# Every instruction tied to its predecessor in the source: the planned order becomes each engine's order

## The chip, the cores and the metric

The kernel runs on one core of a Trainium2 chip. A core has a matrix engine (PE, whose weight loads are listed apart as PEld), a vector engine (DVE), an activation engine (ACT), a general engine (POOL), and a queue engine (SP). Each runs its own stream of instructions in the order in which they stand in that stream, and semaphores tie the streams together. Transfers between the chip's large memory and the on-chip memory are issued from POOL's stream (loads) and from SP's (stores). The metric is the device time of one execution in microseconds. Lower is better.

## The reference

Two steps follow each other. The first is attention with a symmetric window of 32 positions, for 8 batches of 8 heads, 576 positions and head dimension 64. The second routes each of the 4608 resulting rows of 512 values to its two best of eight low-rank adapters and adds their result to the row.

```python
scores = scale * np.matmul(q, k.transpose(0, 1, 3, 2))
mask = np.abs(pos[:, None] - pos[None, :]) <= window          # window = 32
attn = softmax(np.where(mask, scores, -1e9))                  # over the last axis
x = np.matmul(attn, v)   # (B, H, S, D) -> rows (B*S, H*D) = (4608, 512)
logits = x @ w_gate                                           # 8 adapters
topk = two largest logits of a row; w = softmax of those two
delta[row] = sum over the two e of  w_e * ((x[row] @ A[e]) @ B[e])   # rank 16
out = x + delta                                               # float32
```

## The kernel before, in words

The work is cut into small tasks with two-letter names, each one function of the kernel. `b` counts the 8 batches, `n` the 4 head pairs of a batch (unit `u = 4b + n`), `t` the three load tiles of a batch, `w` is 0 for q and 1 for k, `T` counts 36 score tiles of 8 blocks (4.5 a batch), and `h` is one of three row groups of a batch.

- Loads, issued from POOL's stream: `LD` (L274) brings one tile of q or k, `LV` (L279) one half of v. Between them POOL also runs the memsets of `init_v` and `init_kq` and the loads of the weights, at fixed places after the 4th, 8th, 10th and 16th load.
- DVE: `RG` (L289) copies a loaded tile into the layout that is transposed next (tile `c` from tile `l`), `SV` (L284) moves a half of v into place (tile `vbd`), `MU` (L350, L351) divides an attention product by its row sums into `x`, `XE` (L369) copies the transposed x out of PSUM into `xT`, `G1` and `G2` (L394 to L415) are the routing, and `OB` (L446) copies one of the three output groups.
- PE: `TR` (L297) transposes a copied tile, `SC` (L317, L323) computes a score tile with its mask, `PV` (L341) multiplies by v, `TX` (L363) transposes x, `PZ` (L377) computes logits and the first adapter product, `TZ` (L422) transposes the gated result, and `PD` (L432, L435) makes the second adapter product plus x.
- ACT: `EQ` (L303) and `EK` (L311, two copies) take the transposed q and k out of PSUM, `EX` (L328) is the exponential of a score tile, `GA` (L402) the exponential of the gate, `ZE` (L426) a copy, and `OB` (L444) copies two output groups of a batch.
- Stores `ST` (L452) are issued from SP's stream.

PSUM is used as three wide buffers W and two narrow ones T. A task that fills one waits until the task before it on that buffer has been read. There are seven load buffers for each of q and k (a load waits for the `RG` of the tile seven places before it) and three v buffers (a load of v waits for the products of the batch three before it).

`plan()` is a small list scheduler in the kernel's own Python. With a table of costs, the due times of `OFF` and the buffers above it makes one list of all tasks, `order`, and gives each PSUM task its buffer. The kernel then calls the task functions in that list's order, so the source order of instructions is the plan's order. That is not yet the order in which an engine runs them: when the tile framework's context ends, its own scheduler sorts each engine's instructions by its own estimate of when their inputs are ready, as far as data dependencies allow. Only that sorted order reaches the chip. The loop that traces the instructions is

```python
    for t in order:
        do[t.key[0]](*t.key[1:])
```

Of the kernel before, what the change touches and what calls it, by code (L numbers as in the profile page):

```python
# [23 lines left out]
J = 8  # L24
# [206 lines left out]
def kernel(  # L231
# [10 lines left out]
    nc = tc.nc  # L242
    assert tuple(q.shape) == (B, H, S, D)
# [28 lines left out]
    def LD(b, w, t):  # L272
        src = (q, k)[w][b].rearrange("(o n) (p j) d -> (n p) o (j d)", o=2, j=J)
        nc.gpsimd.dma_start(out=raw[w][(NT3 * b + t) % NRAW], in_=src[FT * t:FT * t + FT])  # L274

    def LV(b, o):
        src = v[b, 4 * o:4 * o + 4].rearrange("n (a p two) d -> p (n a) (two d)", p=32, two=2)
        p0, c0 = 64 * o, VW * o + V0
        nc.gpsimd.dma_start(out=vbd[b % NV][p0:p0 + 32, :, c0:c0 + 2 * D], in_=src)  # L279

    def SV(b, o):
        d = vbd[b % NV]
        p0, c0 = 64 * o, VW * o + V0
        nc.vector.tensor_copy(out=d[p0 + 32:p0 + 64, :, c0:c0 + D],  # L284
                              in_=d[p0:p0 + 32, :, c0 + D:c0 + 2 * D])
# [14 lines left out]

    def EQ(b, t):
        c0 = QP + J * FT * t
        nc.scalar.copy(  # L303
            out=qTs[b % 2][:, c0:c0 + J * FT].rearrange("p (f j) -> p f j", j=J),
            in_=ps("TR", b, 0, t)[:, 0:J * FT].rearrange("p (j f) -> p f j", j=J))

    def EK(b, t):
        kt = ps("TR", b, 1, t)[:, 0:J * FT].rearrange("p (r j a f) -> p a r f j", r=2, j=4, f=8)
        for o in range(2):
            dst = kTs[b % 2][64 * o:64 * o + 64, BT * t:BT * t + BT, 64 * o:64 * o + 64]  # L310
            nc.scalar.copy(out=dst.rearrange("p a (r f j) -> p a r f j", r=2, j=4),  # L311
                           in_=kt[64 * o:64 * o + 64])

    def SC(T):
        p = ps("SC", T).rearrange("p (i c) -> p i c", c=128)
        for i in range(0, TB, 4):
            nc.tensor.matmul(out=p[:, i:i + 4], lhsT=maskT, rhs=bcast(ident, 1, 4),  # L317
                             start=True, stop=False)
        for i in range(TB):
            u, a = divmod(TB * T + i, NB)  # L320
            b, n = divmod(u, NP)
            c0 = S * n + 64 * a
            nc.tensor.matmul(  # L323
                out=p[:, i], lhsT=kTs[b % 2][:, NB * n + a, :],
                rhs=qTs[b % 2][:, c0:c0 + 128], start=False, stop=(i % 4 == 3))

    def EX(T):
        nc.scalar.activation(out=PTs[T % NPT][:, :, 64:192],  # L328
                             in_=ps("SC", T).rearrange("p (i c) -> p i c", c=128),
                             func=AF.Exp, scale=1.0 / float(D) ** 0.5)  # L330

    def PV(u):
        b, n = divmod(u, NP)
        po = ps("PV", u)
        for g in range(NG):
            ops = [(a, off) for a, off in ((2 * g - 1, 128), (2 * g, 64), (2 * g + 1, 0))
                   if 0 <= a < NB]
            for i, (a, off) in enumerate(ops):
                T, sl = divmod(NB * u + a, TB)
                rhs = vbd[b % NV][:, NB * n + a].rearrange("p (o c) -> p o c", o=2)  # L340
                nc.tensor.matmul(  # L341
                    out=po[:, GS * g:GS * g + 2 * VD], lhsT=PTs[T % NPT][:, sl, off:off + 128],
                    rhs=rhs[:, :, V0 - 1:V0 + D], start=(i == 0), stop=(i == len(ops) - 1))

    def MU(u):
# [12 lines left out]
    def TX(b, h):  # L358
        tp = ps("TX", b, h)
        for g in gs(h):  # L360
            for c in range(4):
                c0 = 512 * (g % 2) + 128 * c
                nc.tensor.matmul(out=tp[:, c0:c0 + 128],  # L363
                                 lhsT=xs[b % NX][:, g, 128 * c:128 * c + 128],
                                 rhs=ident, is_transpose=True, start=True, stop=True)

    def XE(b, h):
        n = len(gs(h))
        nc.vector.tensor_copy(  # L369
            out=xTs[b % NXT][:, 2 * h:2 * h + n].rearrange("p g c k -> p (g c k)"),  # L370
            in_=ps("TX", b, h)[:, 0:512 * n])

    def PZ(b):
        xT, pz = xTs[b % NXT], ps("PZ", b)
        for g in range(NG):
            for c in range(4):
                nc.tensor.matmul(out=pz[:, GS * g:GS * g + ER + E],  # L377
                                 lhsT=xT[:, g, c, :], rhs=WA_sb[:, c, :],
                                 start=(c == 0), stop=(c == 3))
# [6 lines left out]
    def G1(b):  # L386
        lg = zview(b)[:, :, ER:ER + E]

        def sm(name, shape):
# [4 lines left out]
        nc.vector.tensor_reduce(out=m1, in_=lg, axis=AX.X, op=ALU.max)  # L394
        nc.vector.tensor_tensor(out=is1, in0=lg, in1=bcast(m1, 2, E), op=ALU.is_ge)
        nc.vector.scalar_tensor_tensor(out=lm, in0=is1, scalar=-1e30, in1=lg,
                                       op0=ALU.mult, op1=ALU.add)
        nc.vector.tensor_reduce(out=m2, in_=lm, axis=AX.X, op=ALU.max)
        nc.vector.tensor_tensor(out=dm, in0=m2, in1=m1, op=ALU.subtract)

    def GA(b):
        nc.scalar.activation(out=st[b, "dm"], in_=st[b, "dm"], func=AF.Exp)  # L402

    def G2(b):
# [4 lines left out]
        nc.vector.tensor_tensor(out=is2, in0=lm, in1=bcast(m2, 2, E), op=ALU.is_ge)  # L409
        nc.vector.tensor_scalar(out=s, in0=dm, scalar1=1.0, scalar2=None, op0=ALU.add)  # L410
        nc.vector.reciprocal(out=s, in_=s)
        nc.vector.tensor_tensor(out=is2, in0=is2, in1=bcast(dm, 2, E), op=ALU.mult)  # L412
        nc.vector.tensor_tensor(out=gate, in0=is1, in1=is2, op=ALU.add)
        nc.vector.tensor_tensor(out=gate, in0=gate, in1=bcast(s, 2, E), op=ALU.mult)
        nc.vector.tensor_tensor(  # L415
            out=zss[b % 2], in0=zview(b)[:, :, 0:ER].rearrange("p g (e r) -> p g e r", r=R),
            in1=bcast(gate, 3, R), op=ALU.mult)

    def TZ(b):
        zs = zss[b % 2].rearrange("p g e r -> p g (e r)")  # L420
        for g in range(NG):
            nc.tensor.matmul(out=ps("TZ", b)[:, 128 * g:128 * g + 128], lhsT=zs[:, g],  # L422
                             rhs=ident, is_transpose=True, start=True, stop=True)

    def ZE(b):
        nc.scalar.copy(out=zTs[b % 2].rearrange("p g k -> p (g k)"),  # L426
                       in_=ps("TZ", b)[:, 0:640])

    def PD(b, h):
        pd = ps("PD", b, h).rearrange("p (i c) -> p i c", c=DD)  # L430
        for i, g in enumerate(gs(h)):
            nc.tensor.matmul(out=pd[:, i], lhsT=zTs[b % 2][:, g], rhs=B_sb,  # L432
                             start=True, stop=False)
            for c in range(4):
                nc.tensor.matmul(out=pd[:, i, 128 * c:128 * c + 128],  # L435
                                 lhsT=xTs[b % NXT][:, g, c], rhs=ident,
                                 start=False, stop=(c == 3))

    def OB(b, h):
# [3 lines left out]
        if ts["OB", b, h].eng == "ACT":  # L443
            nc.scalar.copy(out=dst, in_=src)  # L444
        else:
            nc.vector.tensor_copy(out=dst, in_=src)  # L446

    def ST(b, h):
        for i, g in enumerate(gs(h)):
            lo, hi = (32 if g == 0 else 0), (96 if g == NG - 1 else 128)  # L450
            r0 = S * b + 128 * g - 32
            nc.sync.dma_start(out=out[r0 + lo:r0 + hi], in_=obs[(3 * b + h) % NOB][lo:hi, i])  # L452
# [11 lines left out]
    def constants():  # L464
        make_identity(nc, ident)
        nc.gpsimd.memset(mask, 0.0)
        nc.gpsimd.affine_select(out=mask, in_=mask, compare_op=ALU.is_ge, fill=NEG,
                                base=0, channel_multiplier=1,
                                pattern=[[0, 2], [-1, 2], [-2, 32]])
        nc.gpsimd.affine_select(out=mask, in_=mask, compare_op=ALU.is_ge, fill=NEG,  # L470
                                base=64, channel_multiplier=-1,
                                pattern=[[0, 2], [1, 2], [2, 32]])

    def init_kq(i, eng):
        eng.memset(kTs[i][0:64, :, 64:128], 0.0)
        eng.memset(kTs[i][64:128, :, 0:64], 0.0)
        eng.memset(qTs[i][:, 0:QP], 0.0)
        eng.memset(qTs[i][:, QP + NP * S:], 0.0)

    def init_v(i, eng):  # L480
        eng.memset(vbd[i][0:64, :, VW + V0 - 2:VW + V0 + D], 0.0)
        eng.memset(vbd[i][64:128, :, V0 - 2:V0 + D], 0.0)
        eng.memset(vbd[i][0:64, :, V0 - 1:V0], 1.0)
        eng.memset(vbd[i][64:128, :, VW + V0 - 1:VW + V0], 1.0)
# [16 lines left out]
    nc.vector.memset(qTs[0][:, QP + S * 1:QP + S * 1 + 32], 0.0)  # L501
# [49 lines left out]
```

## Time and profile before

| | us |
|---|---|
| median of 3 timed runs | 205.47 (202.04 to 207.04) |
| the profiled execution | 199.97 |
| its span, first to last instruction | 198.0 |
| PE busy, 1720 matmuls | 137.4 (69% of the span) |
| PEld busy | 110.5 (56%) |
| DVE busy | 114.2 (58%) |
| ACT busy | 114.5 (58%) |
| POOL busy | 65.7 (33%) |

All views are of the profiled execution, and their times run from its first instruction. In a timeline each row is a start, a duration, the engine, the line of the kernel, the operation, and out<-in. A bracket names the idle time of the engine just before, and what ended it. Buffer numbers are left out in these views.

### The profile page before, as it was taken

To read this page: it belongs to the slowest core of one execution; us is meant where nothing else is said; L and a number is where in the kernel's file an instruction comes from. 1 tells how busy PE (TensorE), PEld (TensorE's weight loads), DVE (VectorE), ACT (ScalarE), POOL (GpSimd) and SP (SyncE) were. 2 spreads that over 40 slices of the span, in tenths; PEclk is the share of its full clock that TensorE was granted. 3 is DMA by queue.
4 is the path that set the end of the run, shared out by engine and by line. 5 is a ranking of instruction groups with operands and counts; after the bars stand their busy time and mean duration, and the time that the engine had idled before them with its cause. 6 is when DMAs were issued, how large, how long until landed. Compare 5 with 4: busy or idle time off the path is not lost. (4 is left out here: it accounts for less than half of the span.)

```text
span 198.0 us, 4213 instructions
## 1 busy us (share of the span) xinstructions
PE 137.4 (69%) x1720; PEld 110.5 (56%) x1720; DVE 114.2 (58%) x273; ACT 114.5 (58%) x141; POOL 65.7 (33%) x91
## 2 busy tenths in 40 slices
PE   0058395546688655695777979896789899789380
PEld 0046183435586444673565767675667867667250
DVE  6899029060458503956397569377585976676601
ACT  1047900663504975476649867976959899345241
POOL 7999979956202800206220612150000000000000
PEclk9999958585569999789999999999999999999955
DMA  4994999799991996134992499589414006006606
GB/s 65 159 138 75 128 166 42 103 182 197 181 135 9 135 159 158 27 52 78 211 175 46 95 164 257 87 135 255 52 60 181 4 0 239 2 2 237 243 14 224
DMA packets 38770, 24.12 MB, mean 122 GB/s; under 512 B 24800, under 2 KB 34144, under 8 KB 38752
## 3 DMA queue, kind: packets, MB, share of 16 engines
q0 software_dynamic: 33504, 14.43, 64.9%
q1 hardware_dynamic: 5248, 9.44, 13.7%
q8 instruction: 13, 0.21, 0.5%
q14 instruction: 5, 0.04, 0.1%
HBM read 28.85 MB, written 9.44 MB: 193 GB/s over the span
## 5 line engine op out<-in xcount | busy, mean ns | idle before, releaser
L328 ACT ACTIVATE PT<-W 128x1024 f16<-128x1024 f32 x36 | 36.1, 1025 | 12.5 <-PE W L323 10.6
L341 PE MATMUL W<-vbd,PT 128*128 128x130 f16 x416 | 33.9, 240 | 11.0 <-DVE vbd L284 6.0
L311 ACT COPY kT<-T 64x768 f16<-64x768 f16 x48 | 38.1, 793 | 4.9 <-PE T L297 4.6
L297 PE MATMUL T<-ident,c 96*128 96x96 f16 x384 | 25.6, 220 | 17.5 <-DVE c L289 15.1
L341 PEld LDWEIGHTS <-PT 128*128 128x128 f16 x416 | 29.9, 108 | 12.9 <-issue 8.4
L303 ACT COPY qT<-T 128x768 f16<-128x768 f16 x24 | 19.2, 799 | 30.6 <-PE T L297 27.7
L297 PEld LDWEIGHTS <-c 96*128 96x128 f16 x384 | 21.9, 106 | 24.4 <-DVE c L289 19.3
L369 DVE COPY xT<-T 128x1024 f16<-128x1024 f16 (+1 forms) x24 | 13.9, 600 | 31.0 <-PE T L363 20.0
L323 PE MATMUL W<-qT,kT 128*128 128x128 f16 x288 | 25.4, 229 | 6.1 <-ACT kT L311 5.2
L317 PE MATMUL W<-ident,mask 128*128 128x512 f16 x72 | 24.2, 420 | 6.5 <-ACT PT L328 4.0
L274 POOL DMA_DIRECT2D l<-in_q_dram x24 | 16.6, 690 | 36.3 <-DVE is L412 12.0
L323 PEld LDWEIGHTS <-kT 128*128 128x128 f16 x288 | 20.0, 103 | 12.2 <-ACT kT L311 4.5
L351 DVE TENSOR_TENSOR x<-W,rc 128x640 f16<-128x640 f32 x32 | 26.2, 820 | 0.8
L289 DVE COPY c<-l 96x1024 f16<-96x1024 f16 x48 | 25.8, 573 | 0.3
L350 DVE RECIPROCAL rc<-W 128x10 f32<-128x10 f32 x32 | 6.9, 215 | 27.9 <-PE W L341 23.5
L279 POOL DMA_DIRECT2D vbd<-in_v_dram x16 | 13.5, 845 | 25.4 <-PE W L341 23.2
L444 ACT COPY ob<-W 128x1024 f32<-128x1024 f32 x16 | 16.3, 1016 | 8.5 <-PE W L435 5.7
L432 PE MATMUL W<-B_sb,zT 128*128 128x512 f16 x40 | 16.4, 410 | 3.3 <-ACT ob L444 0.9
L435 PEld LDWEIGHTS <-xT 128*128 128x128 f16 x160 | 13.3, 104 | 8.5 <-issue 4.5
L435 PE MATMUL W<-ident,xT 128*128 128x128 f16 x160 | 17.3, 231 | 0.0
L363 PE MATMUL T<-ident,x 128*128 128x128 f16 x160 | 13.7, 230 | 4.1 <-DVE xT L369 1.5
L274 POOL DMA_DIRECT2D l<-in_k_dram x24 | 15.7, 653 | 2.3 <-DVE c L289 1.7
(55 smaller groups left out, 129.4 us busy)
## 6 DMA issues: line engine op xcount, KB each, us to landing
out_dram<-ob SPq DMA_DIRECT2D x24, 256.0 KB, 2.7
l<-in_q_dram POOLq DMA_DIRECT2D x24, 192.0 KB, 7.0
l<-in_k_dram POOLq DMA_DIRECT2D x24, 192.0 KB, 7.4
vbd<-in_v_dram POOLq DMA_DIRECT2D x16, 288.0 KB, 8.1
out_dram<-ob SPq DMA_DIRECT2D x16, 192.0 KB, 2.4
WA_sb<-in_moe_A_dram POOLq DMA_DIRECT2D x4, 32.0 KB, 7.9
B_sb<-in_moe_B_dram POOLq DMA_DIRECT2D x1, 128.0 KB, 4.8
WA_sb<-in_moe_w_gate_dram POOLq DMA_DIRECT2D x1, 8.0 KB, 5.4
```

What stands on the lines that cost most here:

```text
L274: nc.gpsimd.dma_start(out=raw[w][(NT3 * b + t) % NRAW], in_=src[FT * t:FT * t + FT])
L289: nc.vector.tensor_copy(out=cst[w][i % NCAST], in_=raw[w][i % NRAW].rearrange("p o (j d) -> p j o d", j=J))
L297: nc.tensor.matmul(out=tp[:, FT * slot:FT * slot + FT], lhsT=src[:, j, :], rhs=ident[0:FT, 0:FT], is_transpose=True, start=True, stop=True)
L303: nc.scalar.copy(out=qTs[b % 2][:, c0:c0 + J * FT].rearrange("p (f j) -> p f j", j=J), in_=ps("TR", b, 0, t)[:, 0:J * FT].rearrange("p (j ...
L311: nc.scalar.copy(out=dst.rearrange("p a (r f j) -> p a r f j", r=2, j=4), in_=kt[64 * o:64 * o + 64])
L317: nc.tensor.matmul(out=p[:, i:i + 4], lhsT=maskT, rhs=bcast(ident, 1, 4), start=True, stop=False)
L323: nc.tensor.matmul(out=p[:, i], lhsT=kTs[b % 2][:, NB * n + a, :], rhs=qTs[b % 2][:, c0:c0 + 128], start=False, stop=(i % 4 == 3))
L328: nc.scalar.activation(out=PTs[T % NPT][:, :, 64:192], in_=ps("SC", T).rearrange("p (i c) -> p i c", c=128), func=AF.Exp, scale=1.0 / floa ...
L341: nc.tensor.matmul(out=po[:, GS * g:GS * g + 2 * VD], lhsT=PTs[T % NPT][:, sl, off:off + 128], rhs=rhs[:, :, V0 - 1:V0 + D], start=(i == 0 ...
L351: nc.vector.tensor_tensor(out=xs[b % NX].rearrange("p g (h n d) -> p g h n d", h=2, n=NP)[:, :, :, n], in0=pog[:, :, :, 1:VD], in1=bcast(r ...
L432: nc.tensor.matmul(out=pd[:, i], lhsT=zTs[b % 2][:, g], rhs=B_sb, start=True, stop=False)
L435: nc.tensor.matmul(out=pd[:, i, 128 * c:128 * c + 128], lhsT=xTs[b % NXT][:, g, c], rhs=ident, start=False, stop=(c == 3))
```

## The change

`tc.keep_in_program_order` takes an instruction and adds a scheduling edge to the instruction that was traced before it on the same engine. The edge fixes the order of issue. It adds no semaphore and no wait. The change puts this call around every instruction that the kernel itself emits. The planner, its costs and due times, the buffers and the instructions stay as they were. The two instructions of the helper `make_identity` at the start are not wrapped. One added line moves the later line numbers by one (L289 is L290 in the changed kernel).

```diff
     nc = tc.nc
+    keep = tc.keep_in_program_order
...
     def RG(b, w, t):
         i = NT3 * b + t
-        nc.vector.tensor_copy(out=cst[w][i % NCAST],
-                              in_=raw[w][i % NRAW].rearrange("p o (j d) -> p j o d", j=J))
+        keep(nc.vector.tensor_copy(out=cst[w][i % NCAST],
+                              in_=raw[w][i % NRAW].rearrange("p o (j d) -> p j o d", j=J)))
...
-            nc.tensor.matmul(
+            keep(nc.tensor.matmul(
                 out=tp[:, FT * slot:FT * slot + FT], lhsT=src[:, j, :],
-                rhs=ident[0:FT, 0:FT], is_transpose=True, start=True, stop=True)
+                rhs=ident[0:FT, 0:FT], is_transpose=True, start=True, stop=True))
...
-        nc.vector.reciprocal(out=rc, in_=pog[:, :, :, 0])
-        nc.vector.tensor_tensor(
+        keep(nc.vector.reciprocal(out=rc, in_=pog[:, :, :, 0]))
+        keep(nc.vector.tensor_tensor(
             out=xs[b % NX].rearrange("p g (h n d) -> p g h n d", h=2, n=NP)[:, :, :, n],
-            in0=pog[:, :, :, 1:VD], in1=bcast(rc, 3, D), op=ALU.mult)
+            in0=pog[:, :, :, 1:VD], in1=bcast(rc, 3, D), op=ALU.mult))
...
```

The same wrapping stands in every other task function, in the memsets, and in the weight loads. The order of loads on POOL and of stores on SP is the same before and after. On PE the 180 tasks were run in 225 pieces before (a task cut by another counts as two), and run in 180 whole ones now. On DVE it was 175 pieces and is 144, on ACT 117 and 116.

The first place is on DVE at the start. Names ending in 89 to 91 are copied q tiles (`c`), those in 92 to 94 copied k tiles; `l_3` to `l_6` are the load buffers of batch 1 (3 to 5) and of batch 2's first tile (6). An `rc` row and the `x` row behind it are one `MU`. Before:

```order
L284 COPY vbd_64<-vbd_64 32x36x64
L350 RECIPROCAL rc<-W_107 128x10
L351 TENSOR_TENSOR x_95<-W_107,rc 128x10x64
L350 RECIPROCAL rc<-W_108 128x10
L351 TENSOR_TENSOR x_95<-W_108,rc 128x10x64
L350 RECIPROCAL rc<-W_107 128x10
L351 TENSOR_TENSOR x_95<-W_107,rc 128x10x64
L289 COPY c_0_89<-l_3_78 96x1024
L289 COPY c_0_92<-l_3_85 96x1024
L289 COPY c_1_90<-l_4_79 96x1024
```

The same place on DVE in the changed kernel:

```order
L285 COPY vbd_64<-vbd_64 32x36x64
L290 COPY c_0_89<-l_3_78 96x1024
L290 COPY c_0_92<-l_3_85 96x1024
L351 RECIPROCAL rc<-W_107 128x10
L352 TENSOR_TENSOR x_95<-W_107,rc 128x10x64
L290 COPY c_1_90<-l_4_79 96x1024
L290 COPY c_1_93<-l_4_86 96x1024
L351 RECIPROCAL rc<-W_108 128x10
L352 TENSOR_TENSOR x_95<-W_108,rc 128x10x64
L351 RECIPROCAL rc<-W_107 128x10
L352 TENSOR_TENSOR x_95<-W_107,rc 128x10x64
```

The first two copies of batch 1 stood behind three `MU` of batch 0, and now stand ahead of all of them.

The second place is on DVE where batch 2's copies begin. Before, the first of them (from `l_6_81`) stood in the middle of batch 0's routing `G2`, of which these are the last rows:

```order
L351 TENSOR_TENSOR x_96<-W_107,rc 128x10x64
L410 TENSOR_SCALAR s<-dm 128x5
L412 TENSOR_TENSOR is_620<-is_620,dm 128x40
L411 RECIPROCAL s<-s 128x5
L413 TENSOR_TENSOR gate<-is_579,is_620 128x40
L289 COPY c_0_89<-l_6_81 96x1024
L414 TENSOR_TENSOR gate<-gate,s 128x40
L415 TENSOR_TENSOR zs_99<-W_108,gate 128x640
L289 COPY c_0_92<-l_6_88 96x1024
L289 COPY c_1_90<-l_0_75 96x1024
L289 COPY c_1_93<-l_0_82 96x1024
```

In the changed kernel the same copies on DVE stand here (`xT` rows are `XE` of batch 0, the `MU` of `x_96` are units 4 and 5):

```order
L370 COPY xT_97<-T_109 128x1024
L290 COPY c_0_89<-l_6_81 96x1024
L351 RECIPROCAL rc<-W_108 128x10
L352 TENSOR_TENSOR x_96<-W_108,rc 128x10x64
L370 COPY xT_97<-T_110 128x1024
L370 COPY xT_97<-T_109 128x512
L290 COPY c_0_92<-l_6_88 96x1024
L290 COPY c_1_90<-l_0_75 96x1024
L290 COPY c_1_93<-l_0_82 96x1024
L351 RECIPROCAL rc<-W_106 128x10
L352 TENSOR_TENSOR x_96<-W_106,rc 128x10x64
L395 TENSOR_REDUCE m_576<-W_108 128x5
```

All four copies now stand ahead of batch 0's routing, and the routing is not cut by them any more.

The third place is on ACT behind batch 0's `ZE` (`zT`), where batch 2's last q and k tiles leave PSUM. Before:

```order
L426 COPY zT_101<-T_110 128x640
L328 ACTIVATE PT_72<-W_107 128x8x128
L328 ACTIVATE PT_73<-W_108 128x8x128
L444 COPY ob_103<-W_107 128x1024
L303 COPY qT_67<-T_109 128x768
L311 COPY kT_69<-T_110 64x12x64 x2
```

And on ACT in the changed kernel:

```order
L427 COPY zT_101<-T_110 128x640
L329 ACTIVATE PT_72<-W_107 128x8x128
L304 COPY qT_67<-T_109 128x768
L312 COPY kT_69<-T_110 64x12x64 x2
L445 COPY ob_103<-W_107 128x1024
L329 ACTIVATE PT_73<-W_108 128x8x128
```

`EQ` and `EK` moved from behind one `EX` and one `OB` to ahead of both.

## Rows read from the trace of the kernel before

**Rows 1.** The page's line of busy time, share and instructions.

```profile
PE 137.4 (69%) x1720; PEld 110.5 (56%) x1720; DVE 114.2 (58%) x273; ACT 114.5 (58%) x141; POOL 65.7 (33%) x91
```

**Rows 2.** Windows cut at batches' last MU: length, busy, PE clock, DMA, GB/s.

```profile
41.90:65.90 24.00, 16.53 (x176) 13.63 (x176) 12.20 (x33) 10.70 (x15) 7.64 (x12) 0.72 1.10 136
65.90:91.50 25.60, 17.74 (x232) 14.37 (x231) 11.55 (x31) 17.72 (x22) 5.88 (x9) 0.93 0.64 95
91.50:111.40 19.90, 14.54 (x216) 12.03 (x215) 13.74 (x35) 12.84 (x17) 5.94 (x9) 1.00 0.82 130
111.40:129.10 17.70, 15.23 (x215) 12.28 (x212) 10.64 (x30) 13.94 (x18) 5.31 (x9) 1.00 0.98 165
...
164.50:179.10 14.60, 12.38 (x169) 10.05 (x168) 9.81 (x27) 8.20 (x11) 0.00 (x0) 1.00 0.19 65
179.10:198.00 18.90, 10.29 (x99) 7.38 (x99) 6.24 (x18) 5.96 (x7) 0.00 (x0) 0.73 0.51 184
```

**Rows 3.** Timeline of DVE, 17 to 66 us: start, duration, engine, line.

```profile
28.01 0.22 DVE L350 RECIPROCAL rc<-W 128x10 f32<-128x10 f32 x1 [8.35 <-PE W L341]
...
31.75 3.21 DVE L289 COPY c<-l 96x1024 f16<-96x1024 f16 x3
...
41.05 0.82 DVE L351 TENSOR_TENSOR x<-W,rc 128x640 f16<-128x640 f32 x1
...
61.72 0.42 DVE L289 COPY c<-l 96x1024 f16<-96x1024 f16 x1
...
65.02 0.82 DVE L351 TENSOR_TENSOR x<-W,rc 128x640 f16<-128x640 f32 x1
65.88 0.75 DVE L284 COPY vbd<-vbd 32x2304 f16<-32x2304 f16 x1
```

**Rows 4.** Timeline of ACT and of POOL, 28 to 40 us.

```profile
34.93 0.80 ACT L303 COPY qT<-T 128x768 f16<-128x768 f16 x1 [9.93 <-PE T L297]
...
31.66 2.08 POOL L482 MEMSET vbd<- 64x2376 f16 x1
```

**Rows 5.** Load tiles `l` in 34 to 37 us: durations min/median/max, starts, landing.

```profile
L274 POOL DMA_DIRECT2D l<-in_q_dram x2: 637/710/784, 34.3 to 35.7; - x2
L274 POOL DMA_DIRECT2D l<-in_k_dram x2: 639/641/643, 35.1 to 36.3; - x2
...
DMA to landing us min/median/max: 3.5/4.8/6.0
```

**Rows 6.** The page's DMA issues: line, count, size, median us to landing.

```profile
l<-in_q_dram POOLq DMA_DIRECT2D x24, 192.0 KB, 7.0
```

**Rows 7.** Timeline of PE, 54 to 167 us: durations at 1.2 GHz (first) and 2.4.

```profile
54.98 2.98 PE L341 MATMUL W<-vbd,PT 128*128 128x130 f16 x26 [1.33 <-DMA l<-in_k_dram]
...
156.22 1.34 PE L377 MATMUL W<-WA_sb,xT 128*128 128x136 f16 x20
...
158.50 0.50 PE L297 MATMUL T<-ident,c 96*128 96x96 f16 x8
158.84 0.60 PE L317 MATMUL W<-ident,mask 128*128 128x512 f16 x2
159.27 0.61 PE L323 MATMUL W<-qT,kT 128*128 128x128 f16 x8
...
161.40 0.45 PE L422 MATMUL T<-ident,zs 128*128 128x128 f16 x5 [0.23 <-DVE zs L415]
161.69 0.91 PE L341 MATMUL W<-vbd,PT 128*128 128x130 f16 x13
...
166.28 0.61 PE L363 MATMUL T<-ident,x 128*128 128x128 f16 x8
```

**Rows 8.** The chain that ended last, at the last batch's routing: start, duration.

```profile
184.48 0.21 DVE m L394
...
185.61 0.22 ACT dm L402
...
186.63 0.83 DVE zs L415
```

More of the change, by code (lines that the diff above doesn't have):

```diff
@@ L310, in EK @@
             dst = kTs[b % 2][64 * o:64 * o + 64, BT * t:BT * t + BT, 64 * o:64 * o + 64]
-            nc.scalar.copy(out=dst.rearrange("p a (r f j) -> p a r f j", r=2, j=4),
-                           in_=kt[64 * o:64 * o + 64])
+            keep(nc.scalar.copy(out=dst.rearrange("p a (r f j) -> p a r f j", r=2, j=4),
+                           in_=kt[64 * o:64 * o + 64]))
     def SC(T):
@@ L316, in SC @@
         for i in range(0, TB, 4):
-            nc.tensor.matmul(out=p[:, i:i + 4], lhsT=maskT, rhs=bcast(ident, 1, 4),
-                             start=True, stop=False)
+            keep(nc.tensor.matmul(out=p[:, i:i + 4], lhsT=maskT, rhs=bcast(ident, 1, 4),
+                             start=True, stop=False))
         for i in range(TB):
@@ L376, in PZ @@
             for c in range(4):
-                nc.tensor.matmul(out=pz[:, GS * g:GS * g + ER + E],
+                keep(nc.tensor.matmul(out=pz[:, GS * g:GS * g + ER + E],
                                  lhsT=xT[:, g, c, :], rhs=WA_sb[:, c, :],
-                                 start=(c == 0), stop=(c == 3))
+                                 start=(c == 0), stop=(c == 3)))
     st = {}
@@ L421, in TZ @@
         for g in range(NG):
-            nc.tensor.matmul(out=ps("TZ", b)[:, 128 * g:128 * g + 128], lhsT=zs[:, g],
-                             rhs=ident, is_transpose=True, start=True, stop=True)
+            keep(nc.tensor.matmul(out=ps("TZ", b)[:, 128 * g:128 * g + 128], lhsT=zs[:, g],
+                             rhs=ident, is_transpose=True, start=True, stop=True))
     def ZE(b):
-        nc.scalar.copy(out=zTs[b % 2].rearrange("p g k -> p (g k)"),
-                       in_=ps("TZ", b)[:, 0:640])
+        keep(nc.scalar.copy(out=zTs[b % 2].rearrange("p g k -> p (g k)"),
+                       in_=ps("TZ", b)[:, 0:640]))
     def PD(b, h):
@@ L443, in OB @@
         if ts["OB", b, h].eng == "ACT":
-            nc.scalar.copy(out=dst, in_=src)
+            keep(nc.scalar.copy(out=dst, in_=src))
         else:
-            nc.vector.tensor_copy(out=dst, in_=src)
+            keep(nc.vector.tensor_copy(out=dst, in_=src))
     def ST(b, h):
@@ L471, in constants @@
+        keep(nc.gpsimd.affine_select(out=mask, in_=mask, compare_op=ALU.is_ge, fill=NEG,
                                 base=64, channel_multiplier=-1,
-                                pattern=[[0, 2], [1, 2], [2, 32]])
+                                pattern=[[0, 2], [1, 2], [2, 32]]))
     def init_kq(i, eng):
[L475 to L478, printed above, removed]
+        keep(eng.memset(kTs[i][0:64, :, 64:128], 0.0))
@@ L480, in init_v @@
+        keep(eng.memset(kTs[i][64:128, :, 0:64], 0.0))
+        keep(eng.memset(qTs[i][:, 0:QP], 0.0))
+        keep(eng.memset(qTs[i][:, QP + NP * S:], 0.0))
     def init_v(i, eng):
[L481 to L484, printed above, removed]
+        keep(eng.memset(vbd[i][0:64, :, VW + V0 - 2:VW + V0 + D], 0.0))
@@ L486, in init_p @@
+        keep(eng.memset(vbd[i][64:128, :, V0 - 2:V0 + D], 0.0))
+        keep(eng.memset(vbd[i][0:64, :, V0 - 1:V0], 1.0))
+        keep(eng.memset(vbd[i][64:128, :, VW + V0 - 1:VW + V0], 1.0))
     def init_p(i, eng):
-        eng.memset(PTs[i][:, :, 0:64], 0.0)
-        eng.memset(PTs[i][:, :, 192:256], 0.0)
+        keep(eng.memset(PTs[i][:, :, 0:64], 0.0))
+        keep(eng.memset(PTs[i][:, :, 192:256], 0.0))
     def weights():
         for c in range(4):
-            nc.gpsimd.dma_start(out=WA_sb[:, c, 0:ER],
-                                in_=moe_A.transpose([1, 0, 2])[128 * c:128 * c + 128])
@@ L498 @@
+        keep(nc.gpsimd.dma_start(out=B_sb, in_=moe_B.rearrange("e r d -> (e r) d")))
     loads = 0
@@ L500 @@
     init_p(0, nc.vector)
-    nc.vector.memset(qTs[0][:, QP + S * 1:QP + S * 1 + 32], 0.0)
+    keep(nc.vector.memset(qTs[0][:, QP + S * 1:QP + S * 1 + 32], 0.0))
     init_v(0, nc.vector)
```

86 lines of the change are left out of this document (43 added, 43 removed).

## Prediction, made before the changed kernel was run

> **What bounds the kernel now.** I read the page's busy line first, then the windows, then the timelines of the first 70 us. The busy line shows that nothing is full: PE is busy for 69% of the span, DVE and ACT for 58% each [rows 1]. ACT's 114.5 us are 14.3 us for each of the 8 batches, and no engine but PE needs more. The time is therefore lost in waits, and the windows show where.
>
> They are cut where a batch's last MU ends (at 41.87 and 65.84 us for the first two, from the starts and durations of those rows [rows 3]). Batches 1 to 3 took 24.0, 25.6 and 19.9 us. The last four took 67.7 us together (111.4 to 179.1), a mean of 16.9, the very last 14.6 [rows 2]. The early batches are the slow ones, although PE, DVE and ACT are less busy in them: ACT works 10.7 of the 24.0 us of batch 1 [rows 2]. Behind the last MU lies a tail of 18.9 us.
>
> The timelines show what the early batches wait for. DVE stood idle for 8.35 us ahead of the first MU, at 28.01, and the first three copies of batch 1 came after three MUs, at 31.75 [rows 3]. ACT could take nothing meanwhile: its copy of q waited 9.93 us for the transpose that needed that copy [rows 4]. The next batch repeats this. Four loads of batch 2 were issued between 34.3 and 36.3 us, and the last of them, the slowest, landed 6.0 us later, at 42.3 [rows 5]. The first DVE copy of that batch ran at 61.72 [rows 3]. A tile lay ready for some 20 us behind work that waited for something else. So what sets the end is the order in which DVE and PE take their work, and with it the start of each batch.
>
> **The change part by part.** No instruction and no wait is added, so the change costs nothing by itself. PE's, DVE's and ACT's rows move, POOL's loads and SP's stores keep their order, so only two things need costing: when batch 1 is finished, and how long each later batch then takes.
>
> *To the end of batch 1's last MU.* In the new order DVE runs batch 1's first two copies behind the second v move, without waiting for the attention product, and batch 2's first four stand ahead of batch 0's routing. The chain to the last MU of batch 1 then hangs on a transfer that does not move: the batch-2 tile that lands at 42.3. POOL issued it without an idle gap, from a fixed list of memsets and loads. Behind that landing DVE has one copy (0.42 [rows 3]), one MU (0.22 and 0.82 with a gap, 1.07 [rows 3]), the routing G1 (184.48 to 185.61, 1.13 [rows 8]), another MU (1.07), and G2 (1.85: the same chain from 185.61 to 187.46, with the 0.22 of ACT's GA in place of the one row of G2 that needs no GA [rows 8]). That makes 42.3 + 5.54 = 47.84. PE then has, in its new row, TZ 0.45, one SC (158.84 to 159.88, 1.04), TR 0.50 and PV 0.91 [rows 7]: 50.74. The last MU ends at 51.8, where it ended at 65.84 before. The other inputs are earlier by the same walk: batch 1's last two copies cannot start before POOL's memset ends at 33.74 [rows 4], its predecessors' products follow at 35 to 37, and PZ of batch 0 ends at about 42, ahead of the G1 that reads it at 43.8. **Gain 14.0 us.**
>
> Two things bound this stage from above. The first is the clock. PE was granted 0.72 of full speed in 41.9 to 65.9 us and 1.00 from 91.5 us on [rows 2]. At the lower level of 1.2 GHz a PV took 1.49 us (2.98 for two) against 0.91 at 2.4 [rows 7]. The four PE steps above would take 4.75 instead of 2.90 us, so 53.7. I take full speed: the new order gives PE 8 SC, 8 PV, 16 TR and the rest of batch 0 between 21 and 52 us, at these durations about 23 of 31 us, as much as the 14.5 of 19.9 us that were run at 1.00 [rows 2].
>
> The second is POOL. Some six copies and two v moves now run while POOL is still busy with memsets and issues, where three copies ran before. Those three took 3.21 us together beside a memset, where one alone takes 0.42 [rows 3], so the two engines do hinder each other. The issues beside the same copies took 0.784 us at most against 0.637 [rows 5]. By these rows the new copies cost POOL about 0.15 us each, 1.2 in all, and I charge nothing, since in 19 to 30 us POOL mostly issues loads. The Trainium skill's page "SBUF — State Buffer", section "Who interferes with whom", says more against the change: a vector copy in a two-port mode and a POOL instruction exclude each other for the whole instruction, whichever began first. By that rule each copy (0.42) and each v move (0.75) could hold POOL back in full, 4.0 us, and the tile would land at 46.3. The rows do not show this for issues; they show it for a copy that waits behind a memset. It would make this stage 55.8 instead of 51.8. Without that sentence the upper bound of the stage is 53.7 + 1.2 = 54.9.
>
> *Each later batch.* I walk one batch in the new order. On PE, behind the last MU: TX 0.61, SC 1.04, TX 0.61, a short TX 0.4, SC 1.04 (its buffer is free once ACT has done EQ, EK and OB, at about the same time), two TR 1.0, two PV 1.82, PZ 1.34 [rows 7]: 7.9 us. On DVE behind PZ: G1 1.13, a v move 0.75 [rows 3], a copy 0.42, MU 1.07, a copy 0.42, G2 1.85, a v move 0.75, MU 1.07: 7.5 us. So 15.3 us, with no slack in it. Below stands ACT's 14.3 [rows 1]. Above stands 16.9, what the old order reached in the last four batches, when PE's clock was full and loads were ahead [rows 2]. I take 16.2, nearer the old order's rate than the slackless walk would have it. Six batches make 97.2 us, where they took 113.2 before (65.9 to 179.1). **Gain 16.0 us.** ACT's move of EQ and EK ahead of EX and OB is inside this walk: it brings the second SC forward and puts one EX later, which is covered while PE runs TX and SC. Were it not, that PV would wait for the EX, and the batch would come nearer to 16.9.
>
> *The tail.* Its rows stand almost as before: a chain of routing, TZ, ZE, PD, OB and ST of the last batch. 18.9 us [rows 2], no gain.
>
> Sum: 51.8 + 97.2 + 18.9 = 167.9 us of span, and with the 1.97 us that lie around the span before (199.97 - 198.0), 169.9. The profiled execution of before stands 2.7% below the median of its runs (205.47). I see no row that explains that difference, and carry half of it: 172.
>
> **The rivals.** *(a) The start is won, the pace is not.* The transfers could set the pace: in the window 111.4 to 129.1 the DMA engines were busy at a share of 0.98, at 165 GB/s, and the batch took 17.7 us [rows 2]. At that pace the sum is 51.8 + 106.2 + 20.9 = 178.9, some 184 at the runs' level (times 205.47 / 199.97). If nothing but the start is won, it is 199.97 - 14.0 = 186, or 191. For it: a batch's stores fall together with loads. Against it: the batch before ran 19.9 us at a share of 0.82, so the pace does not follow the share, and loads are issued over two batches ahead.
>
> *(b) No difference.* The early batches could be slow through something that the order does not touch, such as the two narrow PSUM buffers or PE's half clock. Then the six batches would need 21.2 us each (51.8 + 127 + 20.9 = 200), the mean of batches 1 to 3 before being 23.2 [rows 2]. Against it: the tile that lay ready for 20 us. That the call does nothing is excluded by the order of the built program.
>
> *(c) Slower.* An order that is fixed can stop the whole DVE stream at one late load. The place is the copy of a load tile that now stands ahead of MU and of routing. A load takes a median of 7.0 us from issue to landing [rows 6]. If every batch waited through one such landing, it would take 15.3 + 7.0 = 22.3 us, and the sum would be 51.8 + 133.8 + 20.9 = 206.5, or 212 at the runs' level. It decides from 6.6 us of wait a batch on. For it: in the walk, the copy of batch 2 does wait for its landing, at 42.3. Against it: from batch 3 on, a tile's buffer is freed seven tiles ahead, some 35 us at 15.3 us for three tiles, five times the landing.
>
> *(d) The pace is ACT's own*, 14.3 us: 51.8 + 85.8 + 20.9 = 158.5, to 163 at the runs' level.
>
> **How the numbers follow.** The forecast has 0.62: two gains that rest on waits seen in the rows. (a) has 0.20, (b) 0.07, (c) 0.06, (d) 0.05. Faster by over 2% is the forecast with (a) and (d), 0.87. 2% is about what a measurement of this kernel can tell from no change. The range goes from 163, just under the slackless pace of 15.3 in the profiled execution (51.8 + 91.8 + 20.9 = 164.5) and the upper end of (d), to 190, nearly the end of (a) at the runs' level. That leaves out (b), (c) and part of (d).
>
> **What would show it.** In the profile after: the first two copies of L290 ahead of the first L352, before 22 us; no wait of 9.9 us of ACT for a transpose; batch 2's first copy near 38 us; the eighth MU ending near 52 us; later windows of four MUs of 15 to 17 us, with PE's clock near 1.00 from 25 us on; a tail of about 19 us. An eighth MU later than 56 would show the first step wrong, windows of over 18 us the second. A DVE that waits on landings in each batch would be (c). DMA shares near 1 beside DVE or PE waits on loads would be (a).

## The result, and the profile after

| | before | after |
|---|---|---|
| median of 4 timed runs, us | 203.75 (199.17 to 207.04) | 158.78 (158.36 to 160.94) |
| ratio after / before | | 0.791 (95% interval 0.777 to 0.805) |
| the profiled execution, us | 199.97 | 158.86 |
| its span, us | 198.0 | 156.9 |

The changed kernel takes 21% less time. The ratio is taken from the faster of the two states that the runs fall into (199.17 and 202.04 us before, all but the 160.94 after). The direction was forecast, the size was not: 158.8 lies below the range of 163 to 190. The two profiled executions differ by 41.1 us, and the ends of the batches' last MU split that:

| stretch | before | after | predicted |
|---|---|---|---|
| start to the end of the eighth MU (batch 1's last) | 65.85 | 51.12 | 51.8 |
| the six batches behind it | 113.23 | 86.22 | 97.2 |
| the tail | 18.9 | 19.6 | 18.9 |

The start gave back 14.7 us, as worked out. The six batches gave 27.0, where 16.0 were expected.

The page's busy line, with the same instructions as in [rows 1]:

```profile
PE 123.2 (79%) x1720; PEld 103.7 (66%) x1720; DVE 119.8 (76%) x273; ACT 113.1 (72%) x141; POOL 67.1 (43%) x91
```

The work is the same and its shares have grown, since the span is shorter. PE lost 14.2 us of busy time: its mean granted clock went from 0.896 to 0.954, and its busy time holds waits inside a task too. ACT lost 1.4 us, and DVE gained 5.6, most of it in its 48 copies of load tiles (654 ns on average against 573). The windows after, cut like [rows 2] at the batches' last MU, with batches 2 to 7 together in the last row:

```profile
35.40:51.10 15.70, 14.68 (x196) 13.08 (x195) 12.67 (x34) 11.05 (x15) 11.96 (x16) 0.85 1.26 167
51.10:65.10 14.00, 13.26 (x202) 11.24 (x200) 11.99 (x32) 13.85 (x19) 7.50 (x11) 1.00 1.46 206
65.10:79.80 14.70, 12.75 (x200) 11.15 (x200) 12.74 (x34) 12.14 (x17) 6.54 (x9) 1.00 1.43 211
79.80:95.30 15.50, 14.75 (x222) 12.43 (x219) 12.64 (x34) 14.80 (x19) 5.91 (x10) 1.00 1.29 227
95.30:109.50 14.20, 12.91 (x205) 11.35 (x204) 11.72 (x31) 11.81 (x16) 1.99 (x3) 1.00 0.96 162
109.50:124.90 15.40, 14.62 (x226) 12.61 (x224) 12.59 (x33) 14.83 (x19) 0.00 (x0) 1.00 0.24 84
124.90:137.30 12.40, 11.71 (x169) 9.87 (x166) 9.60 (x26) 8.32 (x10) 0.00 (x0) 1.00 0.24 84
137.30:156.90 19.60, 10.48 (x104) 7.57 (x101) 6.27 (x19) 6.03 (x8) 0.00 (x0) 0.81 0.51 181
51.10:137.30 86.20, 80.01 (x1207) 68.65 (x1206) 71.29 (x184) 75.76 (x96) 21.94 (x31) 1.00 0.95 164
```

Every batch from the third on now takes 14.0 to 15.5 us, the last one 12.4. Before, they took 25.6, 19.9 and then 16.9 on average. In the windows from 51.1 to 124.9 PE, DVE and ACT are each busy for over 80%, all three at once. The longer windows hold more matmuls (x222, x226 against x200, x205) and more of ACT: 36 score tiles over 8 batches are 4.5 a batch.

The row for the same six batches before, in the same view:

```profile
65.90:179.10 113.20, 90.30 (x1263) 73.79 (x1261) 71.17 (x187) 81.78 (x102) 19.68 (x27) 0.98 0.62 112
```

It has 56 matmuls and six ACT instructions more. The planned order has done that work by its eighth MU, although it reaches it 14.7 us earlier.

The timeline of DVE after, of the places shown in [rows 3]:

```profile
19.98 0.84 DVE L290 COPY c<-l 96x1024 f16<-96x1024 f16 x2
24.02 0.22 DVE L351 RECIPROCAL rc<-W 128x10 f32<-128x10 f32 x1 [3.20 <-PE W L342]
28.95 5.50 DVE L290 COPY c<-l 96x1024 f16<-96x1024 f16 x2
38.28 0.42 DVE L290 COPY c<-l 96x1024 f16<-96x1024 f16 x1 [1.06 <-DMA l<-in_q_dram]
42.17 0.49 DVE L290 COPY c<-l 96x1024 f16<-96x1024 f16 x1 [0.52 <-DMA l<-in_k_dram]
50.29 0.83 DVE L352 TENSOR_TENSOR x<-W,rc 128x640 f16<-128x640 f32 x1
```

Batch 1's first two copies run ahead of the first MU (19.98, before 22 as forecast), batch 2's first copy runs at 38.28 (forecast 38), and the copy on which the sum hung starts at 42.17, when its tile has landed. On ACT the 9.93 us wait of [rows 4] is gone. The same copy of q, after:

```profile
23.76 0.81 ACT L304 COPY qT<-T 128x768 f16<-128x768 f16 x1
```

### The profile page after: what moved, and what is told of

It is laid out like the page before. It is cut to its first block, busy times and chain, and to the rows that moved or that the text cites. A ratio compares the mean times of both kernels' runs of the same rounds, so it can differ in the third digit from the quotient of the medians.

```text
span 156.9 us, 4220 instructions
## 1 busy us (share of the span) xinstructions
PE 123.2 (79%) x1720; PEld 103.7 (66%) x1720; DVE 119.8 (76%) x273; ACT 113.1 (72%) x141; POOL 67.1 (43%) x91
## 4 chain that ended last, share of the span: by engine, by line
PE 39%; DVE 18%; POOL 16%; DMA 10%; ACT 7%; issue 7%; SPq 0%; POOLq 0%; ACTq 0%; DVEq 0%
PE W L342 6%; PE W L324 5%; PE W L318 5%; DVE x L352 5%; PE W L433 5%; POOL l L275 5%; PE W L436 5%; PE T L364 4%; DMA vbd<-in_v_dram 4%; PE T L298 4%; DMA l<-in_k_dram 3%; POOL vbd L482 3%; DVE zs L416 3%; ACT kT L312 2%; PE W L378 2%
## 5 line engine op out<-in xcount | busy, mean ns | idle before, releaser
L298 PEld LDWEIGHTS <-c 96*128 96x128 f16 x384 | 20.8, 104 | 18.6 <-DVE c L290 16.8
L290 DVE COPY c<-l 96x1024 f16<-96x1024 f16 x48 | 30.4, 654 | 2.1 <-DMA l<-in_q_dram 1.3
L342 PE MATMUL W<-vbd,PT 128*128 128x130 f16 x416 | 29.9, 225 | 0.8 <-ACT PT L329 0.6
L342 PEld LDWEIGHTS <-PT 128*128 128x128 f16 x416 | 26.4, 100 | 1.3 <-issue 1.3
L324 PEld LDWEIGHTS <-kT 128*128 128x128 f16 x288 | 19.4, 99 | 9.5 <-issue 1.0
L324 PE MATMUL W<-qT,kT 128*128 128x128 f16 x288 | 22.4, 222 | 0.2 <-ACT kT L312 0.2
L318 PE MATMUL W<-ident,mask 128*128 128x512 f16 x72 | 22.2, 391 | 0.2 <-DVE x L352 0.2
L445 ACT COPY ob<-W 128x1024 f32<-128x1024 f32 x16 | 16.2, 1015 | 6.8 <-PE W L436 4.4
L275 POOL DMA_DIRECT2D l<-in_k_dram x24 | 16.4, 684 | 6.5 <-DMA l<-in_k_dram 2.8
L275 POOL DMA_DIRECT2D l<-in_q_dram x24 | 15.7, 653 | 2.9 <-issue 1.2
L285 DVE COPY vbd<-vbd 32x2304 f16<-32x2304 f16 x16 | 13.9, 868 | 0.5
```

The lines of the kernel that those rows point to most:

```text
L275: keep(nc.gpsimd.dma_start(out=raw[w][(NT3 * b + t) % NRAW], in_=src[FT * t:FT * t + FT]))
L290: keep(nc.vector.tensor_copy(out=cst[w][i % NCAST], in_=raw[w][i % NRAW].rearrange("p o (j d) -> p j o d", j=J)))
L298: keep(nc.tensor.matmul(out=tp[:, FT * slot:FT * slot + FT], lhsT=src[:, j, :], rhs=ident[0:FT, 0:FT], is_transpose=True, start=True, stop ...
L318: keep(nc.tensor.matmul(out=p[:, i:i + 4], lhsT=maskT, rhs=bcast(ident, 1, 4), start=True, stop=False))
L324: keep(nc.tensor.matmul(out=p[:, i], lhsT=kTs[b % 2][:, NB * n + a, :], rhs=qTs[b % 2][:, c0:c0 + 128], start=False, stop=(i % 4 == 3)))
L342: keep(nc.tensor.matmul(out=po[:, GS * g:GS * g + 2 * VD], lhsT=PTs[T % NPT][:, sl, off:off + 128], rhs=rhs[:, :, V0 - 1:V0 + D], start=(i ...
```

## Experiments

The runs of before beside these kernels had 203.96 us (beside the first four), 204.28 (the next four) and a median of 202.5 (the last four). All but the last kernel have a single time, that of the profiled execution, so differences of 2 or 3 us between them say little by themselves. Their stage times in the trace say more. The time of before in the tables is that of its own profiled execution.

### Which engine's order carries the gain

The call is kept on some engines alone:

```diff
-    keep = tc.keep_in_program_order
+    pinned = (mybir.EngineType.DVE,)      # or PE; Activation; PE and DVE
+    def keep(i):
+        return tc.keep_in_program_order(i) if i.ins.engine in pinned else i
```

> Only DVE's instructions are tied to their predecessors; the scheduler orders PE and ACT. Theory A (the loss of the old order is DVE's: copies of landed tiles behind MUs): nearly the whole gain is here, 160 to 168 us, and the eighth MU ends near 52 us. Theory B (the loss is PE's: SC and PV ahead of TR, tasks cut in pieces): PE still runs 218 pieces, the gain is small, 180 to 195 us.

> Only PE's instructions are tied; the scheduler orders DVE and ACT. Theory B: nearly the whole gain, 160 to 168 us. Theory A: DVE keeps part of its old order (161 pieces), 175 to 195 us.

> Only ACT's instructions are tied; DVE is run in 175 pieces and PE in 210, much as before. Theories A and B both expect little: 190 to 205 us. If ACT's order were the cause it would come near 160.

> PE and DVE are tied, ACT, POOL and SP are free. Both theories expect the whole gain, 157 to 162 us, as ACT's order by itself should not matter.

| tied | time | eighth MU ends | six batches |
|---|---|---|---|
| none (before) | 199.97 | 65.85 | 113.2 |
| DVE | 183.64 | 55.40 | 106.8 |
| PE | 176.65 | 50.23 | 105.3 |
| ACT | 193.85 | 62.83 | 111.2 |
| PE and DVE | 163.85 | 53.07 | 88.7 |
| all (after) | 158.86 | 51.12 | 86.2 |

The six batches in the windows of the kernel tied on PE alone,

```profile
50.20:155.60 105.40, 87.08 (x1210) 73.46 (x1207) 70.95 (x185) 77.17 (x96) 22.12 (x32) 0.94 0.78 136
```

and of the one tied on PE and DVE:

```profile
53.10:141.80 88.70, 82.05 (x1207) 70.24 (x1207) 71.23 (x183) 76.21 (x96) 20.72 (x30) 0.98 0.88 155
```

Neither of the two theories, that DVE's order carries the gain or that PE's does, holds alone. The start is won in full with PE tied alone, where DVE's stream came out with batch 1's first two copies ahead of the first MU by itself, and to two thirds with DVE tied alone (10.4 us). The pace is not. PE or DVE alone leaves the six batches at 105 to 107 us, both bring them to 88.7, with nearly the same number of instructions. Part of the 105 to 107 can be PE's clock, 0.94 in these windows of both kernels; but the kernel with only the start tied, in the next section, had 1.00 there and still took 99.3. So the pace comes with the two orders together. Pairs with ACT were not tried.

The kernel tied on PE and DVE lies above the 157 to 162 us that were expected of it. Its start accounts for 2 us: the last of batch 2's first four tiles landed at 44.05 instead of 42.15, and the eighth MU ended 9.0 us behind the landing in both kernels. The other 2.5 us lie in the six batches. Whether ACT's order is worth them, a single run does not show.

### Start and pace taken apart

The call is applied up to the eighth MU only, or from there on only:

```diff
+    pin = [True]                          # late only: [False]
+    def keep(i):
+        return tc.keep_in_program_order(i) if pin[0] else i
     for t in order:
         do[t.key[0]](*t.key[1:])
+        if t.key == ("MU", 7):
+            pin[0] = False                # late only: True
```

> Instructions are tied up to the last MU of batch 1 in the source, later ones are free. If start and pace are separate gains: the eighth MU ends near 51 us, and the six later batches go at the old order's rate of its last four batches, 16.9 us, so 51 + 101 + 20 + 2 = 174 us (up to 186 with the old 113 us for them). If the start alone had caused everything (later batches were slow only because the loads were late and PE's clock low), the six batches take 86 to 90 us and it comes to 159 to 163.

> The reverse: free up to the last MU of batch 1 in the source, tied from there on. If start and pace are separate gains: the eighth MU ends near 66 us as before, then six batches at the new 14.4 us, so 66 + 86 + 20 + 2 = 174 us. If the pace needs the early start (loads issued in time), it is 180 or more.

With the start tied alone: 172.43, eighth MU at 52.31, then 99.3 us for the six batches, 16.55 each:

```profile
52.30:151.60 99.30, 84.30 (x1207) 69.52 (x1206) 68.20 (x183) 75.98 (x95) 21.97 (x30) 1.00 0.81 141
```

With the rest tied alone: 180.77, eighth MU at 65.83, then 20.59 us for the next batch and 72.1 for the last five, where the fully tied kernel takes 72.2 (65.11 to 137.34). Those two stretches in the windows of the kernel that is tied late:

```profile
65.80:86.40 20.60, 17.05 (x256) 14.29 (x255) 14.40 (x36) 18.95 (x25) 6.92 (x10) 1.00 0.83 135
86.40:158.50 72.10, 66.76 (x1007) 57.41 (x1007) 58.99 (x153) 61.96 (x78) 12.46 (x18) 1.00 0.73 135
```

Start and pace can each be won without the other, but they overlap. Of the 27.0 us that the six batches gave, the tied start alone brings 13.9 (113.2 to 99.3; the work done ahead is part of it, since its row has the same 1207 matmuls as after), and the tied rest alone 20.5 (113.2 to 92.7). The run tied late took some 7 us more than the 174 that were expected of separate gains. By its time alone, 180.77, it would fall under the other expectation, a pace that needs the early start. Its rows say otherwise: the last five batches ran at the new pace, and the first row shows where the 7 us went: 256 matmuls and 25 ACT instructions in that batch, against 202 and 19 of the fully tied kernel from 51.1 to 65.1. The free start had left that work undone, and ACT alone is busy for 18.95 of the 20.6 us. The run tied early answers the prediction's question about the old order: even with a won start and the clock at full speed this free order needs 16.55 us a batch, close to the 16.9 of before. Its last batches have before's periods (18.72, 16.65 and 14.59 against 18.73, 16.65 and 14.59). So 16.9 was that order's own cost, not slack that any order has.

### What sets the new pace

Work is taken off one engine at a time: the mask matmuls of SC (PE), the second of EK's copies from batch 2 on (ACT), SV from batch 3 on (DVE), then PE and ACT together, then all three.

```diff
 def SC(T):                                # less PE
-        for i in range(0, TB, 4):
-            keep(nc.tensor.matmul(out=p[:, i:i + 4], lhsT=maskT, rhs=bcast(ident, 1, 4),
-                             start=True, stop=False))
...
-                rhs=qTs[b % 2][:, c0:c0 + 128], start=False, stop=(i % 4 == 3)))
+                rhs=qTs[b % 2][:, c0:c0 + 128], start=True, stop=True))
 def EK(b, t):                             # less ACT
-        for o in range(2):
+        for o in range(2 if b < 2 else 1):
 def SV(b, o):                             # less DVE
+        if b >= NV:
+            return
```

> The changed kernel without the 72 mask matmuls (the window mask is left out of the scores): PE has 15.5 us less to do, 1.9 us a batch. If PE alone sets the pace of 14.4 us, the time falls by 10 us or more, to below 149. If a chain through PE and DVE sets it, two masks a batch lie on that chain, about 0.9 us, 6 in all, 153. If ACT at 14.1 us a batch stands right behind PE, it falls by 1 to 3 us only, 156 to 158.

> The changed kernel with the second copy of EK left out from batch 2 on (half of k is then stale): ACT has 14.2 us less to do, 2.4 us a batch. If PE sets the pace: no change, 157 to 160 us. If ACT sets it: down by 8 us or more, below 151.

> The changed kernel with the v move (SV) left out from batch 3 on (half of v is then stale): DVE has 7.5 us less to do in five batches. If DVE alone sets the pace of 14.4 us: down by 5 us or more, 153 us or less. If no engine alone sets it: 156 to 160 us.

> The changed kernel without the mask matmuls and without the second copy of EK from batch 2 on (mask left out, half of k stale): PE 1.9 and ACT 2.4 us a batch lighter. If PE and ACT are equally close to the pace and stand in for each other: 12.5 us a batch for PE, 11.7 for ACT, 14.0 at most for DVE with the waits between its dependent steps, so 150 to 155 us. If DVE or a chain that goes through DVE sets it: 156 to 160 us, no change.

> All three lightened (no mask, second EK left out from batch 2 on, SV left out from batch 3 on). If the pace is that of three engines of nearly equal load: near 13 us a batch, 148 to 152 us. If the transfers set it (loads at about 11 us a batch and stores beside them): no change, 156 to 160 us.

| less work on | time | six batches | PE busy in them | DVE | ACT |
|---|---|---|---|---|---|
| none (after) | 158.86 | 86.2 | 80.0 | 71.3 | 75.8 |
| PE | 158.18 | 85.6 | 73.8 | 71.0 | 75.5 |
| ACT | 160.58 | 86.3 | 79.6 | 71.4 | 63.8 |
| DVE | 157.46 | 85.1 | 79.5 | 63.9 | 75.6 |
| PE and ACT | 154.18 | 80.2 | 70.1 | 70.7 | 62.5 |
| PE, ACT and DVE | 151.72 | 77.0 | 69.8 | 63.2 | 62.0 |

The row of the kernel with less ACT work, whose last periods stay at 15.44, 14.23, 15.44 and 12.39 us against 15.45, 14.22, 15.44 and 12.40:

```profile
52.30:138.60 86.30, 79.63 (x1206) 68.58 (x1207) 71.36 (x183) 63.79 (x79) 20.72 (x31) 1.00 0.94 162
```

and of the one with less on all three:

```profile
53.50:130.50 77.00, 69.77 (x1160) 64.05 (x1157) 63.22 (x173) 62.03 (x80) 20.18 (x29) 1.00 1.02 178
```

By busy time, taking 12 us from ACT gave nothing in the six batches, 6 us from PE gave 0.6, and 7 us from DVE gave 1.1. (The kernel with less ACT work is slower as a whole through its start: its eighth MU ended at 52.26.) PE and ACT together gave 6.0, all three 9.2. So no engine sets the pace by itself: with one made lighter, another closes the chain. The chains of the fifth batch show it. After, it reaches TZ (L423) by way of ACT, whose EQ, EK, GA and EX fill it from 84.85 us on:

```profile
89.72 1.03 ACT PT L329
90.79 0.91 PE W L342 x13
91.70 0.43 PE T L423 x5
```

With less ACT work it reaches TZ by way of DVE's routing:

```profile
92.04 0.83 DVE zs L416
92.87 0.05 issue
92.92 0.45 PE T L423 x5
```

TZ starts 11.87 and 11.83 us behind the last MU of the batch before (79.83 and 81.09), so both ways take equally long. (The second chain comes to DVE from a load that landed at 90.62. DVE had been busy right up to it.) Of the pairs only PE with ACT was tried. Nor do the transfers set the pace: with all three lightened the same loads and stores run at a higher rate (178 against 164 GB/s), and the batches take 12.8 us. The Trainium skill's page "Perfetto Trace Analysis", section "Identifying the Most-Contended Engine", advises to optimize the engine with the highest occupancy first, and for PE not to go by its matmuls' busy time but, among others, by that of its weight loads. In the row of the six batches after, that engine is ACT (75.76 us, DVE 71.29, PEld 68.65), and here the measurement differs: less ACT work alone brought nothing.

### Moving the memsets off the path of the batch-2 loads

The start still hangs on the tile that lands at 42.15, because POOL issues that load behind two memsets. In this version, which computes everything, the memsets of `init_kq(1)`, `init_v(1)` and `init_v(2)` go from POOL to DVE, and DVE's own first memsets behind its first copies:

```diff
+    behind = {
+        ("RG", 0, 0, 0): [lambda: init_p(0, nc.vector)],
+        ("RG", 0, 1, 0): [lambda: init_v(0, nc.vector)],
+        ("RG", 0, 1, 1): [lambda i=i: init_p(i, nc.vector) for i in range(1, NPT)],
+        ("RG", 0, 1, 2): [lambda: init_kq(1, nc.vector)],
+        ("RG", 1, 1, 0): [lambda: init_v(1, nc.vector)],
+        ("MU", 2): [lambda: init_v(2, nc.vector)],
+    }
     for t in order:
         do[t.key[0]](*t.key[1:])
+        for f in behind.get(t.key, []):
+            f()
```

> The changed kernel with the memsets of the second and third v buffer and of the second q and k buffers taken from POOL to DVE, in gaps of its start, and DVE's own early memsets put behind the first copies. All of the computation is kept. If the start is set by POOL (loads queue behind memsets, and copies wait for memsets): the load that ends the wait of the second batch lands near 34 us, where it landed at 42.2, the eighth MU ends near 43, and the time is 147 to 154 us. If the start is set by the engines: 156 to 160 us.

Median 155.18 (154.80 to 157.79, 4 runs), ratio to before 0.775 (0.767 to 0.782). That is the fastest of all kernels that compute the whole, 3.6 us under the changed kernel, though the two were not compared side by side and the intervals of their ratios overlap. It lies between the two times that were expected (147 to 154, or 156 to 160). The tile landed at 33.83 (expected 34) and the eighth MU ended at 46.52, where 43 was expected. DVE's timeline shows one reason:

```profile
26.46 1.05 DVE L482 MEMSET vbd<- 64x1188 uint32 x1 [0.19 <-issue]
27.79 1.05 DVE L483 MEMSET vbd<- 64x1188 uint32 x1 [0.29 <-issue]
...
29.37 0.84 DVE L285 COPY vbd<-vbd 32x2304 f16<-32x2304 f16 x1
```

The third pair of memsets, put behind MU 2, kept DVE from the v move until 29.37, whose data had landed at 22.7. From 39.1 to 45.8 us the chain that ended last then runs through ACT's copies and exponentials, so the landing is no longer what the start waits for. Another place for the memsets was not tried. The six batches behind the eighth MU took 86.6 us, with the same periods as after (15.45, 14.23, 15.44, 12.40 at the end): an earlier start moves the whole rest, and changes nothing in it.

## Why the prediction was right and wrong

**The start: right.** 51.12 measured, 51.8 predicted, and the steps hold one by one. The landing was put at 42.3 and came at 42.15. In the six other kernels with this order at the start and the memsets in place, the tile landed at 42.1 to 43.3 and the eighth MU ended at 51.1 to 53.5, so a match to 0.7 us is partly chance. (Some of them had less work on an engine.) The chain of work that ended last runs through the same stations as the sum, from the landing on:

```profile
36.98 5.17 DMA l<-in_k_dram
42.17 0.49 DVE c L290
...
42.82 0.82 DVE x L352
...
44.81 0.82 DVE x L352
...
46.63 0.83 DVE zs L416
...
47.51 0.45 PE T L423 x5
47.96 0.43 PE W L318 x2
```

DVE was done at 47.46 (predicted 47.84).

**Hindrance between DVE and POOL: rightly not charged, with some luck.** The two engines do hinder each other. In the load tiles' view of 34 to 37.3 us one issue took 978 ns instead of 630, beside a v move of DVE:

```profile
L275 POOL DMA_DIRECT2D l<-in_k_dram x2: 629/804/978, 35.4 to 37.0; - x2
```

The larger price was on the other side: two copies took 5.50 us instead of 0.84 (DVE's timeline, 28.95), beside these two rows of POOL's timeline:

```profile
29.75 2.12 POOL L482 MEMSET vbd<- 64x2376 f16 x1
31.91 2.26 POOL L483 MEMSET vbd<- 64x2376 f16 x1
```

POOL waited for a landing of v in both kernels, until 28.01 before and 28.02 after. So what it lost ahead of that does not count, and its stream had a gap there (1.03 us before), other than the prediction says. From there to the issue of the last tile's load it lost 0.63 us (36.98 against 36.35), about half of the 1.2 that the rows gave as a bound. The landing did not move back because the transfer then took 5.2 us instead of 6.0, which was not forecast. The 4.0 us that were worked out from the Trainium skill's page "SBUF — State Buffer", section "Who interferes with whom", did not appear. Of two such instructions, the same section states, the one that issues first blocks the other in full. The second copy agrees: it ran from 32.07 to 34.45, and the memset that began ahead of it ended at 34.17. The first does not, as the rows stand: it began at 28.95, ahead of its memset, and still ended behind it, at 32.15.

**PE's clock: wrong, without effect.** It was forecast near 1.00 from 25 us on. The window 35.4 to 51.1 had 0.85, and the page's slices show the fall:

```profile
PE   0024998659988998998699989979999899893480
PEclk9999999975899999999999999999999999999659
```

Slices are 3.9 us wide. In 27 to 35 us, while DVE's two copies stood beside the memsets, PE was busy for only half to two thirds, and the granted clock then fell to 0.5 in the slice from 35.3. It was back before the chain left DVE for PE at 47.5, so the four PE steps ran at full speed.

**Each later batch: the step that failed.** The walk of one batch gave 15.3 us, and 16.2 were taken. Measured were 14.37 on average. Half of the miss is the walk: it added the PE tasks' durations, but consecutive matmul tasks overlap in the timeline of PE. The chain counts each piece only from the end of the one before it to its own end. Batch 2, which took 13.99 us, behind its predecessor's last MU:

```profile
51.15 0.59 PE T L364 x8
51.74 0.43 PE W L318 x2
52.17 0.45 PE W L324 x8
52.62 0.67 PE T L364 x12
53.29 0.49 PE W L318 x2
53.77 0.45 PE W L324 x8
54.22 0.68 PE T L298 x16
54.90 0.76 PE W L342 x13
```

| PE task | predicted | in the chain |
|---|---|---|
| TX | 0.61 | 0.59 |
| SC | 1.04 | 0.88 |
| TX and the short TX | 1.01 | 0.67 |
| SC | 1.04 | 0.93 |
| two TR | 1.00 | 0.68 |
| two PV, to PZ's start at 56.24 | 1.82 | 1.34 |
| PZ | 1.34 | 1.34 |
| together | 7.9 | 6.4 |

The chain of this batch leaves PE behind the first PV and reaches G1 by way of two MU, which end at 57.81, hardly later than PZ. The PZ row is from PE's timeline:

```profile
56.24 1.34 PE L378 MATMUL W<-WA_sb,xT 128*128 128x136 f16 x20
```

DVE's part then ran from 57.74 to 65.11, 7.4 us against 7.5 predicted. The walk is the path of this batch and not of every one: in the fifth, of 15.5 us, the middle of the chain is ACT's, as shown above. The Trainium skill's page "Perfetto Trace Analysis", section "Per-engine timelines", says that a matmul's end is a model and not an observation. The table agrees: the durations add up to 7.9 us, and the stretch that they fill is 6.4.

The other half is the choice of 16.2, "nearer the old order's rate than the slackless walk would have it". That took 16.9 for something that any order pays. The run with only the start tied shows that it belonged to the free order: 16.55 a batch behind the same start, at the same clock. Of the 1.83 us a batch between 16.2 and 14.37, 0.9 are this choice (16.2 - 15.3) and 0.93 the walk (15.3 - 14.37). Over six batches that is 5.4 and 5.6 us, together the 11.0 by which the table differs.

**The tail and the level of the runs.** The tail was 0.7 us longer than assumed, and the start 0.7 us shorter. The 2.1 us that were carried because before's profiled execution lay under the median of its runs fell away: after, the median (158.78) is the profiled execution's time (158.86). Why before's profiled execution lay under that median was not settled.

**The rivals.** (a), transfers set the pace, is refuted: batches of 14 to 15.5 us ran at DMA shares of 1.29 to 1.46 and up to 227 GB/s, far above the 0.98 and 165 of [rows 2]. (b) and (c) are refuted by the time itself; the wait for a landing that (c) feared occurs at 42.17 and not in each batch. (d), 158.5 us with ACT as the bound, has the right number for a wrong reason: 12 us less of ACT's work in the six batches left them at 86.3. ACT is one of several bounds that lie close together: beside lighter PE work the same cut brought 5.4 us (85.6 to 80.2). A time that fits a rival does not show that rival.

## What to carry to other kernels

Where a kernel's own plan is good, a second scheduler that sorts each engine's stream by itself can lose much of it: here the orders of PE and DVE were worth 6 to 8 us of the six batches one by one, and 24.5 together. When a batch is walked by hand, do not count the overlap of consecutive matmul tasks twice, and do not take the old order's best rate as a bound for a new order. Before work is cut from the busiest engine, compare its load with that of the others: where several are close, as here, lightening one can bring nothing.

## What the runs showed of the hardware

- A DVE copy that takes 0.42 us alone took 2.4 and 3.2 us beside POOL's memsets: over all 48 copies the mean was 573 ns before, 654 ns after, and 449 ns where the memsets ran on DVE instead. The memset that takes 2.12 us on POOL (64x2376 f16) takes 1.05 on DVE (64x1188 uint32).
- The transfers ran at 206 to 227 GB/s for 44 us in a row (51.1 to 95.3), beside three engines that were over 80% busy.
- With the order fixed, the last four periods repeat to 0.02 us between kernels: 15.45, 14.22, 15.44, 12.40 after, and within that of these in the runs tied late, with less ACT work, and with the memsets moved.
